# Gated mix of attention and FFN for one token: 384 columns of a w_down block as strips of 16 rows, and two more blocks in the early sum

## Chip, cores and metric

The kernel runs on one core of a Trainium2 chip. The metric is the device time of one execution in microseconds (us), as the median of several runs.

## What is computed

One token x of 1024 numbers goes through attention over a cache and through a gated FFN; a sigmoid gate mixes the two. All is float32. In short, from the reference:

```python
# x (1,1,1024); k_cache, v_cache (1,4,65536,128); wq (1024,4096); wo (4096,1024)
g = sigmoid((x * gate_w).sum(-1))
a = softmax(q @ k.T * 128**-0.5) @ v @ wo          # 32 heads, 8 to each of 4 cached groups
r = x @ w_r
y = (silu(x @ w_gate) * (x @ w_up)) @ w_down       # w_gate, w_up (1024,3584); w_down (3584,1024)
out = g * a + (1 - g) * (x + y * sigmoid(r))
```

The router picks one of one token, so every token is routed. The caches are 268 MB, and all inputs together 346 MB, each read once.

## The kernel before

**The stream.** All inputs are loaded by one queue, SP's, in the order in which they are used, into three large buffers, kbuf, vbuf and wbuf, each of 128 partitions by 64 KB. SP waits until TensorE has finished with a buffer and then issues the next transfer into it (`load`, lines 108 to 111). Keys go to kbuf, values to vbuf, the matrices wq, wo and most of w_down to wbuf. The host packs everything after the caches into one array, `tail`, with one row for each partition.

**Attention** runs over 4 groups of heads in 4 steps each; per group wo is applied and summed into T, a PSUM tile of 128 x 512 (T is never cleared until the end; four quarters of 32 partitions hold partial sums, the first and third for columns 0 to 511 of the output, the second and fourth for columns 512 to 1023; `tiles`, line 151, deals the blocks round).

**FFN.** w_gate and w_up arrive in halves in kbuf and vbuf (lines 210 to 225, two passes). After each pass seven small matmuls S <- row, sel4 (line 224) spread the 3584 results over 128 partitions by 28 columns, one column for each block of 128 rows of w_down. VectorE forms the hidden vector from it, in `hid` and, with zeros around each number so that it can serve as a weight of 32 columns, in `hp` (line 384).

**The end, w_down in 28 blocks** of 128 rows by 1024 columns. Blocks 0 to 15 come in wbuf: VectorE sums blocks 0 to 5 into `t` (the early sum, lines 393 to 398), TensorE takes 6 to 15 into T (line 231), then t (line 233), then blocks 16 to 23 from kbuf (lines 234 to 237). VectorE copies T to `join` (line 400). The rest goes into a second, narrow PSUM tile Y of 128 x 64: blocks 24 and 25, then join itself by a matmul with `selj` that adds T's quarters, then block 26, then block 27 in two pieces (lines 244 to 263). A block in T takes two matmuls of 512 columns, a block in Y sixteen of 64. VectorE transposes Y into `fin` and SP stores it (lines 402 to 404).

TensorE's instructions run in the order written; a wait holds up all behind it. The parts of w_down that go to kbuf are issued together, and TensorE waits for each by its own semaphore `s_part`:

```python
    parts = [4 * D, 4 * D, 2 * D, D] + [4 * CW * (r1 - r0) for r0, r1 in PIECES]
    for k, n in enumerate(parts):
        to = at - down - W
        load(kb[:, to : to + n], tail[:, at : at + n], s_part[k], 0 if k else FFN + 4)
```

Of the kernel before, what the change touches and what calls it, by code (L numbers as in the profile page):

```python
# [4 lines left out]
AF = mybir.ActivationFunctionType  # L5
# [11 lines left out]
W = 16384  # L17
KB = D // P
FB = F // P
FR = F // 8  # L20
FQ = FB // 4
SCALE = DH ** -0.5
XN = 32
JOIN = 24
SUMS = 6
R4 = 4
CW = D // 16
PIECES = ((0, 3), (3, 4))

# [20 lines left out]

def gated_mix(nc, k_t, v_t, wq0, wo_wq, tail, out):
    pe, dve, act, pool = (
# [10 lines left out]
    def sb(name, *shape):  # L63
        return nc.alloc_sbuf_tensor(name, (P, *shape), F32)[:]
# [3 lines left out]
    if nc.sbuf_base % 256:  # L68
# [7 lines left out]
    xp, qp, op, hp = sb("xp", KB, 32), sb("qp", 4 * (32 + HG)), sb("op", HG, 32), sb("hp", FB, 36)  # L76
    hid = sb("hid", FB)
    sel, sel8, sel4, selq, selj = (
        sb("sel", 32), sb("sel8", HG), sb("sel4", 4), sb("selq", 2), sb("selj", 2, 36),
    )  # L80
# [6 lines left out]
    nbs = nb0, nb1  # L87
    xr, fin = sb("xr", KB), sb("fin", 2 * 32)

# [34 lines left out]
    half = KB // 2 * F  # L124
    down = at + 4 * half
    for dst, n, sem, after in (
# [107 lines left out]
    for k in range(2):  # L234
        p.wait_ge(s_part[k], 16)
        d2 = kb[:, 4 * k * D : 4 * (k + 1) * D].rearrange("p (b n) -> p b n", n=D)
        ins = tiles(T, [hp[:, 16 + 4 * k + b, 3:35] for b in range(4)], d2, False, k == 1)
    join_ready = pe(ins)

    def y_row(j, r, lhs, rhs, first=False, last=False):  # L240

        return mm(y[32 * j : 32 * j + 32, :], lhs[:, 3 - r : 35 - r], rhs, first, last)

    later = kb[:, 8 * D : 11 * D].rearrange("p (b j r n) -> p b j r n", b=3, j=4, r=R4)
    for b in range(3):
        if b != 1:
            p.wait_ge(s_part[(2, 0, 3)[b]], 16)
        for r in range(R4):
            for j in range(4):
                y_row(j, r, hp[:, JOIN + b, :], later[:, b, j, r, :], b == r == 0)  # L250
        if b == 1:
            event()
            joined = join.rearrange("p (j r n) -> p j r n", j=2, r=R4)
            for r in range(R4):
                for j in range(4):
                    y_row(j, r, selj[:, j // 2, :], joined[:, j % 2, r, :])
    at = 11 * D
    for k, (r0, r1) in enumerate(PIECES):
        p.wait_ge(s_part[4 + k], 16)
        for r in range(r0, r1):  # L260
            for j in range(4):
                ins = y_row(j, r, hp[:, FB - 1, :], kb[:, at : at + CW], False, r == R4 - 1)
                at += CW
    y_done = pe(ins)

# [95 lines left out]
    for u in range(2):  # L361
        act.wait(pe, FFN + 3 * u + 2)
        if u:
            act.wait(dve)
        a.activation(
            row.rearrange("p (e n) -> p e n", e=2), R.rearrange("p (e n) -> p e n", e=2)[:, :, :FR], AF.Copy
        ).then_inc(to_pe, 1)
        cols = FFN + 3 * u + 3
        if u == 0:
            act.wait(pe, cols)  # L370
            act(a.activation(hid, S[:, :FB], AF.Exp, scale=-1.0))
# [17 lines left out]
    d(v.tensor_mul(hid, S[:, :FB], hid))
    dacc, h = t, hid.rearrange("p (m j) -> p j m", j=4)  # L390
# [50 lines left out]
```

## Time and profile before

| | |
|---|---|
| median of 3 runs | 805.45 us (805.37 to 805.81) |
| the profiled execution | 805.7 us, span 804.4 us |
| TensorE matmuls busy | 396.7 us, 49% of the span |
| VectorE, ScalarE, GpSimd busy | 82.2, 24.9, 2.7 us |
| read from HBM | 346.05 MB, 430 GB/s over the span |
| mean granted clock of TensorE | 0.739 of 2.4 GHz |

The span runs from the first to the last instruction of the program; the profiled execution's time is 1.3 us longer than its span. Busy shares are means over the whole span; the change touches mainly its last 60 us, and times below are counted from the start of the span. TensorE (PE) has its weight loads listed apart (PEld). A float32 matmul appears as two records, so "x40" in the trace is 20 matmuls.

### The profile page before, as it was taken

Reading aid. Unit: us, or ns where it says so; the run is one execution under the profiler, and the core shown is the slowest. Engines: PE = TensorE matmul, PEld = TensorE weight load, DVE = VectorE, ACT = ScalarE, POOL = GpSimd, SP = SyncE. Lnnn points to the kernel's source line nnn. Section 1 sums busy time; section 2 is a strip of 40 time slices with the busy share of each in tenths; the row PEclk is TensorE's granted clock in tenths of the full one; section 3 lists DMA queues with packets and bytes.
Section 4 is the critical chain, followed back from the end, with each engine's and each line's share of the span. In section 5 each row is a group of like instructions: output and inputs, shape, how many; then the busy total and the mean of one; then the engine's idle time right before and its main releaser. Section 6 shows DMA issues by size and latency. Waiting matters only on the chain. (4 is left out here: it accounts for less than half of the span.)

```text
span 804.4 us, 6296 instructions
## 1 busy us (share of the span) xinstructions
PE 396.7 (49%) x2932; PEld 124.3 (15%) x2932; DVE 82.2 (10%) x159; ACT 24.9 (3%) x49; POOL 2.7 (0%) x12
## 2 busy tenths in 40 slices
PE   3444554455544444455445455455444454545556
PEld 1111111111111111111111111111111111111222
DVE  1010101010001010100101010100101010100004
ACT  0000000000000000000000000000000000000000
POOL 1000000000000000000000000000000000000000
PEclk9777677677676776776776777777777777777768
DMA  9999999999999999999999999999999999999997
GB/s 415 420 418 466 417 420 466 417 417 463 424 417 460 427 417 460 427 417 460 427 417 456 430 417 453 433 417 450 433 420 443 440 420 430 437 449 417 451 422 320
DMA packets 7061, 346.13 MB, mean 430 GB/s; under 512 B 912, under 2 KB 1040, under 8 KB 1296
## 3 DMA queue, kind: packets, MB, share of 16 engines
q1 hardware_dynamic: 7056, 346.05, 99.4%
q8 instruction: 4, 0.07, 0.0%
q14 instruction: 1, 0.01, 0.0%
HBM read 346.05 MB, written 0.00 MB: 430 GB/s over the span
## 5 line engine op out<-in xcount | busy, mean ns | idle before, releaser
L149 PE MATMUL S<-kbuf,qp 128*32 128x512 f32 x1024 | 145.2, 730 | 155.6 <-PEq L146 155.6
L149 PE MATMUL A<-vbuf,pt 128*32 128x512 f32 x1024 | 145.2, 730 | 132.3 <-PEq L146 132.3
L149 PEld LDWEIGHTS S<-kbuf,qp 128*32 128x32 f32 x1024 | 40.1, 131 | 257.4 <-issue 257.4
L149 PEld LDWEIGHTS A<-vbuf,pt 128*32 128x32 f32 x1024 | 40.1, 131 | 224.4 <-issue 224.4
L322 DVE TENSOR_REDUCE m<-S 128x1 f32<-128x1024 f32 x16 | 19.6, 1224 | 291.3 <-PE S L149 291.3
L149 PE MATMUL T<-wbuf,op 128*32 128x512 f32 x128 | 21.9, 847 | 24.5 <-PEq L146 24.5
L341 DVE SCALAR_TENSOR_TENSOR acc<-acc,alpha,A 128x512 f32<-128x512 f32 x12 | 9.0, 748 | 169.1 <-PE A L149 169.1
L149 PE MATMUL R<-vbuf,xp 128*32 128x448 f32 x128 | 17.6, 721 | 16.3 <-PEq L146 16.3
L149 PE MATMUL R<-kbuf,xp 128*32 128x448 f32 x128 | 17.5, 716 | 15.6 <-PEq L146 15.6
L334 ACT ACTIVATE t<-S,nb 128x1024 f32<-128x1024 f32 x16 | 17.6, 1099 | 196.8 <-DVE nb L327 196.8
L338 DVE STREAM_TRANSPOSE pt<-t 128x1024 f32<-128x1024 f32 x16 | 19.8, 1239 | 5.1 <-ACT t L334 5.1
L149 PE MATMUL M<-mg,heads 128*128 128x16 f32 x32 | 5.9, 259 | 27.3 <-PEq L143 27.3
L333 ACT ACTIVATE alpha<-nb 128x1 f32<-128x1 f32 x12 | 3.5, 294 | 449.5 <-DVE nb L330 449.5
L149 PE MATMUL R<-wbuf,xp 128*32 128x512 f32 x128 | 16.1, 647 | 0.0
L149 PEld LDWEIGHTS T<-wbuf,op 128*32 128x32 f32 x128 | 5.7, 148 | 37.5 <-issue 37.5
L149 PEld LDWEIGHTS M<-mg,heads 128*128 128x128 f32 x32 | 4.8, 188 | 41.4 <-issue 41.4
L149 PE MATMUL T<-wbuf,hp 128*32 128x512 f32 x40 | 6.1, 771 | 7.5 <-DMA wbuf<-in_tail 7.5
L149 PEld LDWEIGHTS R<-vbuf,xp 128*32 128x32 f32 x128 | 5.4, 140 | 28.6 <-issue 28.6
L149 PEld LDWEIGHTS R<-kbuf,xp 128*32 128x32 f32 x128 | 5.4, 140 | 27.1 <-issue 27.1
L149 PE MATMUL T<-join 128*128 128x512 f32 x2 | 2.0, 1126 | 13.9 <-PEq L143 13.9
L343 DVE COPY acc<-A 128x512 f32<-128x512 f32 x4 | 2.8, 691 | 59.7 <-PE A L149 59.7
L394 DVE SCALAR_TENSOR_TENSOR t<-wbuf,hid,t 128x1024 f32<-128x1024 f32 x6 | 7.7, 1285 | 7.3 <-DMA wbuf<-in_tail 7.1
(74 smaller groups left out, 80.5 us busy)
## 6 DMA issues: line engine op xcount, KB each, us to landing
kbuf<-in_tail SPq DMA_DIRECT2D x2, 7168.0 KB, 31.0
vbuf<-in_tail SPq DMA_DIRECT2D x2, 7168.0 KB, 29.5
wbuf<-in_wq SPq DMA_DIRECT2D x1, 4112.0 KB, 12.6
wbuf<-in_tail SPq DMA_DIRECT2D x1, 4096.0 KB, 38.0
kbuf<-in_tail SPq DMA_DIRECT2D x2, 2048.0 KB, 34.3
kbuf<-in_tail SPq DMA_DIRECT2D x1, 1024.0 KB, 38.5
kbuf<-in_tail SPq DMA_DIRECT2D x1, 512.0 KB, 39.3
kbuf<-in_tail SPq DMA_DIRECT2D x1, 384.0 KB, 39.8
```

The source lines that it names most:

```text
L149: return p.matmul(o, w, r, start=first, stop=last)
L322: d(v.tensor_reduce(m1, S, AX.X, ALU.max))
L333: act(a.activation(alpha, was, AF.Exp, bias=now, scale=-1.0))
L334: act(a.activation(t, S, AF.Exp, bias=now, scale=SCALE, accum_out=sums if i else l1))
L338: tell_pe(v.transpose(pt, t))
L341: d(v.scalar_tensor_tensor(acc, acc, alpha, A, op0=ALU.mult, op1=ALU.add))
L343: d(v.tensor_copy(acc, A))
L394: ins = v.scalar_tensor_tensor(dacc, wb[:, b * D : (b + 1) * D], h[:, 0, b : b + 1], dacc, op0=ALU.mult, op1=ALU.add)
```

## The change

In block 23 of w_down the columns 0 to 383 no longer come with the rest of the block. The host cuts the 128 rows of this piece into eight strips of 16 rows and packs them in a new input, `low`, of four rows with four partitions' data in each. One transfer puts them side by side on partitions 0 to 15 of kbuf; its leading dimension of four has it carried by four DMA engines. It is the first of the transfers into kbuf behind wbuf. Eight matmuls with 16 rows and 384 columns add the strips into T. So that the hidden numbers of block 23 also stand on partitions 0 to 15, eight matmuls of one column are added to each FFN pass, and `hp` and `hid` have 36 columns in place of 28 (they are laid out as four groups of nine).

Blocks 24 and 25 are added into T, ahead of the copy to join, and no longer into Y. Y starts with join. The pieces of the stream behind wbuf are cut anew: the strips, blocks 16 to 19, blocks 20 to 22 and the rest of 23, blocks 24 and 25, block 26 with three quarters of 27, and the last quarter of 27. The strips and blocks 16 to 19 are taken ahead of the early sum t, which stood ahead of block 16.

```diff
-    parts = [4 * D, 4 * D, 2 * D, D] + [4 * CW * (r1 - r0) for r0, r1 in PIECES]
-    for k, n in enumerate(parts):
-        to = at - down - W
-        load(kb[:, to : to + n], tail[:, at : at + n], s_part[k], 0 if k else FFN + 4)
+    n = SUB * MOVED
+    load(kb[:LOW, LAST : LAST + n], low[:, : OWN * n].rearrange("e (q n) -> e q n", q=OWN), s_part[0], FFN + 4)
+    to = 0
+    for k, n in enumerate((4 * D, 4 * D - MOVED, 2 * D, 2 * D - 4 * CW, 4 * CW)):
+        load(kb[:, to : to + n], tail[:, at : at + n], s_part[k + 1])
         at += n
+        to += n
...
         for m in range(FQ):
-            ins = mm(S[:, 4 * m : 4 * m + 4], row[:, m * P : (m + 1) * P], sel4)
+            mm(S[:, 4 * m : 4 * m + 4], row[:, m * P : (m + 1) * P], sel4)
+        j, m = divmod(SPLIT, FQ)
+        for q in range(SUB):
+            at = m * P + q * LOW
+            ins = mm(S[:, FB + q : FB + q + 1], row[:, at : at + P], sel4[:, j : j + 1])
...
     event()
     p.wait_ge(s_down, 16)
+    p.wait_ge(s_part[0], 16)
     d1 = wb.rearrange("p (b n) -> p b n", n=D)
-    tiles(T, [hp[:, b, 3:35] for b in range(SUMS, 16)], d1[:, SUMS:, :], False, False)
+    tiles(T, [flat(hb(b)) for b in range(SUMS, 16)], d1[:, SUMS:, :], False, False)
+    for q in range(SUB):
+        j = q % 2 * 2
+        mm(
+            T[32 * j : 32 * j + 32, :MOVED], flat(hp[:LOW, q % 4 * HB + FQ + q // 4, :]),
+            kb[:LOW, LAST + q * MOVED : LAST + (q + 1) * MOVED], False, False,
+        )
+    p.wait_ge(s_part[1], 16)
+    tiles(T, [flat(hb(16 + b)) for b in range(4)], kb[:, : 4 * D].rearrange("p (b n) -> p b n", n=D), False, False)
     event()
     tiles(T, [ones[:, :32]], t.unsqueeze(1), False, False)
...
+    p.wait_ge(s_part[2], 16)
+    split = flat(hb(SPLIT))
+    at = 7 * D
+    mm(T[:32, MOVED:], split, kb[:, at : at + 512 - MOVED], False, False)
+    mm(T[32:64, :], split, kb[:, at + 512 - MOVED : at + D - MOVED], False, False)
+    at += D - MOVED
+    tiles(T, [flat(hb(20 + b)) for b in range(3)], kb[:, 4 * D : 7 * D].rearrange("p (b n) -> p b n", n=D), False, False)
+    p.wait_ge(s_part[3], 16)
+    join_ready = pe(
+        tiles(T, [flat(hb(24 + b)) for b in range(2)], kb[:, at : at + 2 * D].rearrange("p (b n) -> p b n", n=D), False, True)
+    )
```

On TensorE the end of the program stood like this before (from the first w_down matmul on; T and Y are the PSUM tiles, kbuf and wbuf hold w_down, hp the hidden vector, t the early sum):

```order
L149 MATMUL T<-wbuf,hp 32x512 x20
L149 MATMUL T<-t,ones 32x512 x2
L149 MATMUL T<-kbuf,hp 32x512 x16
L149 MATMUL Y<-kbuf,hp 32x64 x32
L149 MATMUL Y<-join,selj 32x64 x16
L149 MATMUL Y<-kbuf,hp 32x64 x32
```

and now it stands like this, from the same place on:

```order
L157 MATMUL T<-wbuf,hp 32x512 x20
L157 MATMUL T<-kbuf,hp 32x384 x8
L157 MATMUL T<-kbuf,hp 32x512 x8
L157 MATMUL T<-t,ones 32x512 x2
L157 MATMUL T<-kbuf,hp 32x128
L157 MATMUL T<-kbuf,hp 32x512 x11
L157 MATMUL Y<-join,selj 32x64 x16
L157 MATMUL Y<-kbuf,hp 32x64 x32
```

The eight strips and eight matmuls of blocks 16 to 19 have moved between wbuf and t, T has 27 matmuls on kbuf and 1 of 128 columns where it had 16 in all with t behind wbuf, and 32 matmuls into Y ahead of join are gone.

On SP, the queue of transfers, the last ones before the store were (destination <- source, partitions x numbers):

```order
L111 DMA wbuf<-in_tail 128x16384
L111 DMA kbuf<-in_tail 128x4096 x2
L111 DMA kbuf<-in_tail 128x2048
L111 DMA kbuf<-in_tail 128x1024
L111 DMA kbuf<-in_tail 128x768
L111 DMA kbuf<-in_tail 128x256
```

and are now:

```order
L118 DMA wbuf<-in_tail 128x16384
L118 DMA kbuf<-in_low 16x1x3072
L118 DMA kbuf<-in_tail 128x4096
L118 DMA kbuf<-in_tail 128x3712
L118 DMA kbuf<-in_tail 128x2048
L118 DMA kbuf<-in_tail 128x1792
L118 DMA kbuf<-in_tail 128x256
```

The strips stand directly behind wbuf; the 128-row transfers behind them carry 384 numbers a row less in all.

## Rows read from the trace of the kernel before

**Rows 1.** The page: busy time, share of the span and instructions of each engine; then the DMA share in tenths and GB/s in 40 equal slices of the span; then two of the DMA queues, with packets, MB and share of the 16 engines' time.

```profile
PE 396.7 (49%) x2932; PEld 124.3 (15%) x2932; DVE 82.2 (10%) x159; ACT 24.9 (3%) x49; POOL 2.7 (0%) x12
...
PE   3444554455544444455445455455444454545556
...
DMA  9999999999999999999999999999999999999997
GB/s 415 420 418 466 417 420 466 417 417 463 424 417 460 427 417 460 427 417 460 427 417 456 430 417 453 433 417 450 433 420 443 440 420 430 437 449 417 451 422 320
...
q1 hardware_dynamic: 7056, 346.05, 99.4%
q8 instruction: 4, 0.07, 0.0%
```

**Rows 2.** The windows, one full stretch and the end: from and to, length, then busy us and instructions of PE, PEld, DVE, ACT and POOL, and last the granted clock of TensorE, the mean busy share of the 16 DMA engines and GB/s.

```profile
740.00:755.00 15.00, 8.52 (x70) 3.71 (x66) 0.93 (x4) 1.11 (x2) 0.00 (x0) 0.72 1.00 433
...
799.60:800.00 0.40, 0.40 (x17) 0.30 (x18) 0.00 (x0) 0.00 (x0) 0.00 (x0) 1.00 0.91 336
800.00:800.40 0.40, 0.40 (x43) 0.40 (x36) 0.30 (x1) 0.00 (x0) 0.00 (x0) 1.00 0.33 128
...
801.20:801.60 0.40, 0.40 (x44) 0.40 (x37) 0.00 (x0) 0.00 (x0) 0.00 (x0) 1.00 0.15 54
801.60:802.00 0.40, 0.40 (x35) 0.33 (x28) 0.00 (x0) 0.00 (x0) 0.00 (x0) 1.00 0.05 18
802.00:803.00 1.00, 0.60 (x35) 0.44 (x32) 0.25 (x1) 0.00 (x0) 0.00 (x0) 1.00 0.00 0
```

**Rows 3.** The DMA issues of w_down's last parts: destination <- source, queue, count, KB of each, median us from issue to landing.

```profile
kbuf<-in_tail SPq DMA_DIRECT2D x1, 1024.0 KB, 38.5
...
kbuf<-in_tail SPq DMA_DIRECT2D x1, 384.0 KB, 39.8
...
kbuf<-in_tail SPq DMA_DIRECT2D x1, 128.0 KB, 39.7
```

**Rows 4.** The timeline of the end: start, length, engine, line, operation, out<-in, shapes, count of records, and in brackets the idle time before and what ended it.

```profile
760.31 2.70 SPq L111 DMA_DIRECT2D kbuf<-in_tail  x6
...
787.50 7.89 DVE L394 SCALAR_TENSOR_TENSOR t<-wbuf,hid,t 128x1024 f32<-128x1024 f32 x6 [7.08 <-DMA wbuf<-in_tail]
...
787.52 6.12 PE L149 MATMUL T<-wbuf,hp 128*32 128x512 f32 x40 [7.49 <-DMA wbuf<-in_tail]
...
795.54 0.62 PE L149 MATMUL T<-t,ones 128*32 128x512 f32 x2 [1.90 <-PEq L143]
...
795.57 0.62 PE L149 MATMUL T<-kbuf,hp 128*32 128x512 f32 x2
...
795.97 0.62 PE L149 MATMUL T<-t,ones 128*32 128x512 f32 x2
...
796.02 4.00 PE L149 MATMUL T<-kbuf,hp 128*32 128x512 f32 x30
...
800.10 0.69 DVE L400 COPY join<-T 128x512 f32<-128x512 f32 x1 [4.71 <-PE T L149]
...
800.94 0.65 PE L149 MATMUL Y<-join,selj 128*32 128x64 f32 x32
...
801.38 1.22 PE L149 MATMUL Y<-kbuf,hp 128*32 128x64 f32 x64
802.67 0.25 DVE L402 STREAM_TRANSPOSE fin<-Y 128x64 f32<-128x64 f32 x1 [1.88 <-PE Y L149]
```

**Rows 5.** The same timeline around the small matmuls of the FFN passes.

```profile
751.44 8.81 PE L149 MATMUL R<-kbuf,xp 128*32 128x448 f32 x64 [5.36 <-PEq L146]
...
778.34 1.70 PE L149 MATMUL S<-sel,row 128*128 128x4 f32 x14 [1.12 <-PEq L143]
```

**Rows 6.** The waits: engine, tile and line, what it waited for, us in total, times, longest.

```profile
DVE xp L293 <- DMA wbuf<-in_wq: 8.5, 1, 8.5
```

**Rows 7.** The timeline of TensorE's weight loads for the w_down matmuls on wbuf, columns as in rows 4.

```profile
789.23 0.20 PEld L149 LDWEIGHTS T<-wbuf,hp 128*32 128x32 f32 x4 [0.66 <-issue]
790.09 0.20 PEld L149 LDWEIGHTS T<-wbuf,hp 128*32 128x32 f32 x4 [0.66 <-issue]
790.90 0.12 PEld L149 LDWEIGHTS T<-wbuf,hp 128*32 128x32 f32 x4 [0.62 <-issue]
791.33 0.12 PEld L149 LDWEIGHTS T<-wbuf,hp 128*32 128x32 f32 x4 [0.31 <-issue]
...
792.62 0.12 PEld L149 LDWEIGHTS T<-wbuf,hp 128*32 128x32 f32 x4 [0.31 <-issue]
```

**Rows 8.** The windows for the same matmuls, columns as in rows 2.

```profile
787.60:790.80 3.20, 3.20 (x16) 0.71 (x20) 3.13 (x3) 0.00 (x0) 0.00 (x0) 0.50 1.04 445
790.90:793.60 2.70, 2.70 (x28) 0.60 (x20) 2.63 (x3) 0.00 (x0) 0.00 (x0) 1.00 0.93 401
```

**Rows 9.** The timeline of TensorE's weight loads in two FFN bursts: the first of each, and where their distance changes.

```profile
751.40 0.23 PEld L149 LDWEIGHTS R<-kbuf,xp 128*32 128x32 f32 x8 [5.41 <-issue]
...
756.64 0.18 PEld L149 LDWEIGHTS R<-kbuf,xp 128*32 128x32 f32 x4 [0.52 <-issue]
...
768.27 0.23 PEld L149 LDWEIGHTS R<-vbuf,xp 128*32 128x32 f32 x8 [8.82 <-issue]
...
774.02 0.14 PEld L149 LDWEIGHTS R<-vbuf,xp 128*32 128x32 f32 x4 [0.30 <-issue]
```

More of the change, by code (lines that the diff above doesn't have):

```diff
@@ L23 @@
 XN = 32
-JOIN = 24
+JOIN = 26
+SPLIT = 23
 SUMS = 6
-R4 = 4
+RY = 4
+BY = 8 // RY
 CW = D // 16
-PIECES = ((0, 3), (3, 4))
+LOW = 16
+OWN = 4
+SUB = P // LOW
+HB = 7 + SUB // 4
+MOVED = 384
+LAST = 12 * D
 class Flow:
@@ L48, in own, with gated_mix @@
         self.wait(self)
-def gated_mix(nc, k_t, v_t, wq0, wo_wq, tail, out):
+def gated_mix(nc, k_t, v_t, wq0, wo_wq, tail, low, out):
     pe, dve, act, pool = (
@@ L75, in gated_mix @@
     wb = wb[:, :W]
-    xp, qp, op, hp = sb("xp", KB, 32), sb("qp", 4 * (32 + HG)), sb("op", HG, 32), sb("hp", FB, 36)
-    hid = sb("hid", FB)
+    xp, qp, op, hp = sb("xp", KB, 32), sb("qp", 4 * (32 + HG)), sb("op", HG, 32), sb("hp", 4 * HB, 32 + RY)
+    hid = sb("hid", 4 * HB)
     sel, sel8, sel4, selq, selj = (
-        sb("sel", 32), sb("sel8", HG), sb("sel4", 4), sb("selq", 2), sb("selj", 2, 36),
+        sb("sel", 32), sb("sel8", HG), sb("sel4", 4), sb("selq", 2), sb("selj", 2, 32 + RY),
     )
@@ L87, in gated_mix @@
     nbs = nb0, nb1
-    xr, fin = sb("xr", KB), sb("fin", 2 * 32)
+    xr, fin = sb("xr", KB), sb("fin", BY * 32)
     def ps(name, n=512):
@@ L124, in gated_mix @@
     half = KB // 2 * F
-    down = at + 4 * half
     for dst, n, sem, after in (
@@ L149, in mm, with hb, flat @@
         return p.matmul(o, w, r, start=first, stop=last)
+    def hb(b):
+        return hp[:, b // FQ * HB + b % FQ, :]
+    def flat(h):
+        return h[:, RY - 1 : RY + 31]
     def tiles(o, lhs, rhs, first, last, n=512):
@@ L223, in gated_mix, with y_rows @@
         for m in range(FQ):
-            ins = mm(S[:, 4 * m : 4 * m + 4], row[:, m * P : (m + 1) * P], sel4)
+            mm(S[:, 4 * m : 4 * m + 4], row[:, m * P : (m + 1) * P], sel4)
[3 more added lines that the diff above has]
+            ins = mm(S[:, FB + q : FB + q + 1], row[:, at : at + P], sel4[:, j : j + 1])
         pe(ins)
     pe.n = FFN + 6
+    def y_rows(rhs, lhs, lo=0, hi=D // 4, first=False, last=False):
+        n = D // 4 // RY
+        for r in range(RY):
+            c0, c1 = max(lo, r * n), min(hi, r * n + n)
+            for j in range(4 if c0 < c1 else 0):
+                ins = mm(
+                    y[32 * j : 32 * j + 32, c0 - r * n : c1 - r * n], lhs(j)[:, RY - 1 - r : RY + 31 - r],
+                    rhs(j)[:, c0 - lo : c1 - lo], first and r == 0, last and r == RY - 1,
+                )
+        return ins
@@ L232, in gated_mix @@
+    p.wait_ge(s_part[1], 16)
+    tiles(T, [flat(hb(16 + b)) for b in range(4)], kb[:, : 4 * D].rearrange("p (b n) -> p b n", n=D), False, False)
     event()
     tiles(T, [ones[:, :32]], t.unsqueeze(1), False, False)
[L234 to L264, printed above, removed]
+    p.wait_ge(s_part[2], 16)
[3 more added lines that the diff above has]
+    mm(T[32:64, :], split, kb[:, at + 512 - MOVED : at + D - MOVED], False, False)
@@ new lines, in gated_mix, with columns @@
+    at += D - MOVED
[3 more added lines that the diff above has]
+        tiles(T, [flat(hb(24 + b)) for b in range(2)], kb[:, at : at + 2 * D].rearrange("p (b n) -> p b n", n=D), False, True)
+    )
+    at += 2 * D
+    def columns(at, n):
+        return lambda j: kb[:, at + j * n : at + (j + 1) * n]
+    event()
+    y_rows(lambda j: join.rearrange("p (j n) -> p j n", j=2)[:, j % 2, :], lambda j: selj[:, j // 2, :], first=True)
@@ L267, in gated_mix @@
+    p.wait_ge(s_part[4], 16)
+    y_rows(columns(at, D // 4), lambda j: hb(JOIN))
+    at += D
+    edge = D // 4 - CW
+    y_rows(columns(at, edge), lambda j: hb(FB - 1), hi=edge)
+    p.wait_ge(s_part[5], 16)
+    y_done = pe(y_rows(columns(at + 4 * edge, CW), lambda j: hb(FB - 1), lo=edge, last=True))
     pool(gp.memset(ident, 0.0))
@@ L370, in gated_mix @@
             act.wait(pe, cols)
-            act(a.activation(hid, S[:, :FB], AF.Exp, scale=-1.0))
+            act(a.activation(hid, S[:, : 4 * HB], AF.Exp, scale=-1.0))
             dve.wait(act)
@@ L376, in gated_mix @@
             dve.own()
-            d(v.tensor_mul(hid, S[:, :FB], hid))
+            d(v.tensor_mul(hid, S[:, : 4 * HB], hid))
             dve.own()
@@ L388, in gated_mix @@
             )
-    d(v.tensor_mul(hid, S[:, :FB], hid))
+    d(v.tensor_mul(hid, S[:, : 4 * HB], hid))
     dacc, h = t, hid.rearrange("p (m j) -> p j m", j=4)
@@ L401, in gated_mix @@
     dve.wait(pe, y_done)
-    d(v.transpose(fin.rearrange("p (r b) -> p b r", b=2), y))
+    d(v.transpose(fin.rearrange("p (r b) -> p b r", b=BY), y))
     sp.wait_ge(dve.sem, dve.n)
@@ L413 @@
     wq = a["A_wq"].reshape(P, KB, G, HG * DH).transpose(2, 0, 1, 3)
-    turned = lambda w: w.reshape(-1, 4, 32, R4, 2).transpose(0, 1, 3, 4, 2)
+    turned = lambda w: w.reshape(-1, 4, 32, D // P).transpose(0, 1, 3, 2)
     wo = turned(a["A_wo"]).reshape(G, HG, P, D).transpose(0, 2, 1, 3)
     down = turned(a["B_w_down"]).reshape(FB, P, D).transpose(1, 0, 2)
-    last = down[:, -1].reshape(P, 4, R4, CW)
+    last = down[:, -1].reshape(P, 4, D // 4)
+    moved = down[:, SPLIT, :MOVED].reshape(SUB, LOW // OWN, OWN, MOVED).transpose(1, 2, 0, 3).reshape(LOW // OWN, -1)
     vecs = np.zeros((P, XN), np.float32)
@@ L426 @@
             [wo[-1].reshape(P, -1), a["B_w_gate"].reshape(P, -1), a["B_w_up"].reshape(P, -1)]
-            + [down[:, :-1].reshape(P, -1)]
-            + [last[:, :, r0:r1].transpose(0, 2, 1, 3).reshape(P, -1) for r0, r1 in PIECES],
+            + [down[:, :SPLIT].reshape(P, -1), down[:, SPLIT:-1].reshape(P, -1)[:, MOVED:]]
+            + [x.reshape(P, -1) for x in (last[:, :, :-CW], last[:, :, -CW:])],
             axis=1,
         ),
+        "low": np.pad(moved, ((0, 0), (0, D))),
     }
```

6 lines of the change are left out of this document (3 added, 3 removed).

## Prediction

> **What bounds the kernel now.** I read the page first. Its slices show the DMA engines busy in nine tenths or more of every slice but the last, at 415 to 466 GB/s, and TensorE mostly in four or five tenths [rows 1]. So 346 MB are streamed without a pause, and only two things can move the time: the bytes that the slowest of the 16 engines carries, and what follows its last byte.
>
> The second view is the windows. In a full stretch 433 GB/s are moved, 27.1 GB/s by each engine; in the last microseconds the share falls to 0.33 between 800.0 and 800.4, to 0.15, to 0.05, and is zero from 802.0 [rows 2]. A third of 16 is five: eleven engines are done by about 800.2, the other five go on, the last ones for almost 2 us. The landings agree: six transfers are issued in the 2.70 us from 760.31, and the last, of 128 KB, lands 39.7 us after its issue, at about 802.3; the one before it lands 39.8 us after its own, at about 801.9 [rows 3, 4].
>
> The third view is TensorE's timeline of the end [rows 4]. The w_down matmuls on wbuf start at 787.52 and end at 793.64. Then TensorE is idle for 1.90 us, until VectorE's early sum, six steps that end at 795.39, may be added. T ends at 800.02, its copy to join runs from 800.10 for 0.69, the Y matmuls end at 802.60, and the transpose starts at 802.67 [rows 4]. So the last matmuls end 0.3 us behind the last landing, and the transpose and the store behind them do not change. The reader should see two clocks that end together: the stream, and TensorE, with 1.9 us of slack in its middle.
>
> **The stream.** Each of the 128 rows loses 384 columns, 1536 bytes. An engine carries eight rows, so twelve engines lose 12 KB, which is 0.45 us at 27.1 GB/s. The other four carry four rows of 12 KB of the new input, 48 KB, 1.82 us, and end 1.82 - 0.45 = 1.37 us later than they did. If these four are among the eleven that end near 800.2, they now end at about 801.6, and the slowest engine ends at 801.85 in place of 802.3: a gain of 0.45 on the stream. The Trainium skill ("DMA: Bandwidth & Descriptors", section on why a semaphore rises by 16) says that a transfer gets the largest number of engines that divides both leading sizes, here 4 and 16; no row shows such a transfer yet.
>
> **FFN and start.** Eight more matmuls of one column stand in each pass behind the seven that take 1.70 us [rows 5], so at most 1.70 x 8/7 = 1.95 us a pass. In the first pass TensorE then waits 5.36 us for kbuf, in the second VectorE waits 7.08 us for wbuf [rows 4, 5]: cost nothing; without that cover 1.95. A larger zeroing of hp adds under a microsecond to POOL's 2.7 in all, against 8.5 us in which VectorE waits for the first load [rows 1, 6]: nothing; wider operations on hid stand under the same 7.08. SP issues as many transfers behind wbuf as before, over 20 us ahead of their use.
>
> **The wait that moves.** TensorE now waits for wbuf and for the strips before its first w_down matmul, and all of T is queued behind it. The strips lie behind wbuf on four engines. On an early engine wbuf is done 2 us before 787.5, so they land at 787.5 - 2 + 1.82 = 787.3: nothing. On the latest engine they would land at 789.3: a rival below.
>
> **TensorE's sum.** A matmul into 32 rows of T uses one of four column groups, and four go side by side: weight loads come in fours, 0.86 us apart until 790.09 and 0.43 us apart from 790.90 [rows 7], where the granted clock goes from 0.50 to 1.00 [rows 8], from 1.2 to 2.4 GHz. Each matmul is two such passes, so a 512-column one costs its group 0.86 us at 2.4 GHz. Before, a group got five from wbuf and, in the first two groups, one for the early sum and four from kbuf: 5 x 0.86 = 4.3 from 795.54, and the row ends at 800.02, 0.18 later, the run-out of the last. That the groups run on independently is seen at 795.57: matmuls on kbuf start between the two passes on t, which can only be the third and fourth group [rows 4].
>
> Now the first group. From wbuf it is free at 792.62 + 2 x 0.43 = 793.48 as before. Then come four of the eight strips (the strips use groups one and three alone) of 384 columns, no such shape is in the trace; by columns each is 0.75 x 0.86 = 0.64, together 2.57. Bounds: half of it if one pass did, 1.29; and double, 5.15, if the two groups took turns; I take 2.57, since the nearest rows, those on t and kbuf, show groups side by side. Then two from blocks 16 to 19 (1.72), one for the early sum (0.86, ready since 795.4), 128 columns of block 23 (0.21), two from blocks 20 to 22 (1.72), one from block 24 (0.86). Sum 7.94: free at 801.42, with the run-out 801.60, against 800.02. The slack of 1.9 us is filled, and nothing on the way waits for data: the piece with block 24 takes the place of one that landed 38.5 us after its issue, at about 799.7 [rows 3], and the group comes to it at 800.56.
>
> Behind T: copy at 801.68 for 0.69, the first join matmul 0.15 later, as before, at 802.52. Sixteen Y matmuls take 0.44 (the join row starts at 800.94, the next at 801.38) and run out in 0.21 more [rows 4]. The 48 that are left, all data landed, take 3 x 0.44 + 0.21 = 1.53: end at 804.05. Before it was 802.60. So +1.45 us in this execution; dropping 32 Y matmuls for blocks 24 and 25 is counted in it, since they stood ahead of the stream's end.
>
> To that comes the clock. Of the 6.12 us on wbuf the first 3.3 ran at 1.2 GHz [rows 8], and before, the 1.9 us of slack absorbed it; now each microsecond more at 1.2 GHz costs half of one. Other bursts in this trace ran longer before the passes got faster: 751.40 to 756.64 is 5.2 us, 768.27 to 774.02 is 5.7 us [rows 9]. The mean of the three is 4.7, 1.4 more than here, half of which is 0.7. I take 0.6, with bounds of -0.4 and +1.2. **Sum: 1.45 + 0.6 = 2.05 us.** The profiled execution took 805.7 with a span of 804.4; the median of the runs is 805.45, 0.25 under it, and I add the sum to the median: 807.5.
>
> **Rivals.**
> - *TensorE is not the bound.* T would have to end by about 800.0, 1.6 us sooner than summed: with the strips at one pass (1.29 saved) and a slightly earlier clock, or the clock at 2.4 GHz from the start (1.66 saved). Then the end follows the stream. The piece ahead of the last lands at 801.5, the 28 Y matmuls behind it take 7 x 0.11 = 0.77 and the last four 0.11, end at about 802.4: 0.2 to 0.45 sooner than before, 805.1. For it speaks the stream's share of 1.00 everywhere; against it that every term of the sum but the strips is a row. Chance 0.25.
> - *The groups stop at the strips.* If groups two and four may not run on while groups one and three take the strips, group two starts block 16 at 796.05 and has 7 matmuls of 0.86 left, 802.07, and with two run-outs of 0.16 to 0.18 about 802.4 in place of 801.42: another 0.95 us, 808.45. The Trainium skill ("TensorEngine Tiling (Array Packing)", Key Properties) says that a change of tiling mode, not of tile alone, drains TensorE, and a strip of 16 rows has another mode than 128 rows; by that rule it is this case. No row of before has two such shapes without a wait between them. Chance 0.25.
> - *One of the four engines is a late one.* Then the strips land between 788.3 and 789.3, TensorE starts 0.8 to 1.8 us later and T ends as much later, 808.3 to 809.3. No row names the engines; by count alone it would be likely (four of 16 beside five late ones), yet one of the mildly late ones would cost little. Chance 0.15.
>
> **How the numbers follow.** My case has 0.35. It gives 807.5, with its own range of 806.5 to 808.7 from the clock. A measurement of this kernel tells about 0.2%, 1.6 us, from no change: below 807.06 nothing is slower by that. Of my case about three quarters lie above, 0.26; the next two rivals lie above but for a little, 0.38: slower 0.64. The first rival and the rest of my case are within it: 0.33. For a gain over 1.6 us the stream would have to lose all its lateness at once: 0.03. The range must hold the first rival, since it has more than 2 in 10: 805.0 to 809.0 leaves out the upper half of the third rival and little else.
>
> **What would show it.** Right: in TensorE's timeline no gap near 794, a row of sixteen 128x384 passes there, T running past 801, join copied at 801.7 or later, three blocks of Y without a gap, and DMA share zero while they run. The strips in fours 0.32 us apart support the 2.57. Wrong: T ending near 800 and a wait of Y for kbuf (first rival); no block 16 matmul before the last strip ended (second); a first w_down matmul well behind wbuf's landing, VectorE starting its early sum before it (third). One of the four instruction packets [rows 1], if it fell on one of the four engines near the end, would upset the first rival's sum as well.

## The result, and the profile after

The changed kernel takes 810.02 us as the median of six executions (808.83 to 810.33), against 805.46 (805.37 to 805.95) before: a ratio of 1.0052, with a 95% interval of 1.0039 to 1.0065. It is slower by 4.56 us, where 2.05 were forecast; the range to 809.0 does not hold it. Five further executions in a later series had a median of 809.16 (808.85 to 809.38; ratio 1.0046, 1.0032 to 1.0060). One execution of experiment 7 ran in a slower state of the chip (838.67 us) and is in none of the figures below.

The profiled execution took 808.83 us with a span of 807.5. The page's first part answers to [rows 1]:

```profile
PE 408.1 (51%) x2924; PEld 131.4 (16%) x2924; DVE 82.3 (10%) x159; ACT 25.0 (3%) x49; POOL 3.0 (0%) x12
```

TensorE is busy for 11.4 us longer, in part because it ran at the lower clock for longer (below). The timeline of the end, with the columns of [rows 4]:

```profile
776.94 5.64 PE L157 MATMUL S<-sel,row 128*128 128x4 f32 x30 [1.12 <-PEq L151]
...
787.37 7.89 DVE L427 SCALAR_TENSOR_TENSOR t<-wbuf,hid,t 128x1024 f32<-128x1024 f32 x6 [4.38 <-DMA wbuf<-in_tail]
...
788.40 6.05 PE L157 MATMUL T<-wbuf,hp 128*32 128x512 f32 x40 [5.81 <-DMA kbuf<-in_low]
...
794.38 4.62 PE L157 MATMUL T<-kbuf,hp 16*32 16x384 f32 x32
...
798.82 1.03 PE L157 MATMUL T<-t,ones 128*32 128x512 f32 x4
...
799.68 3.60 PE L157 MATMUL T<-kbuf,hp 128*32 128x128 f32 x24
...
803.35 0.69 DVE L433 COPY join<-T 128x512 f32<-128x512 f32 x1 [8.09 <-PE T L157]
...
804.63 1.10 PE L157 MATMUL Y<-kbuf,hp 128*32 128x64 f32 x64
805.79 0.25 DVE L435 STREAM_TRANSPOSE fin<-Y 128x64 f32<-128x64 f32 x1 [1.75 <-PE Y L157]
```

The reader should see three things. VectorE starts its early sum at 787.37, when wbuf is there, but TensorE starts at 788.40, released by the strips (in_low): 0.88 us later than in [rows 4]. From then on the timeline shows TensorE without a gap until T ends. And the copy to join starts at 803.35, 3.25 us later than before and 1.67 later than forecast; what follows it takes as long as forecast (2.38 us to the last Y matmul, 2.37 forecast).

The weight loads of the same execution, with the columns of [rows 7], show how the column groups take the strips:

```profile
790.94 0.22 PEld L157 LDWEIGHTS T<-wbuf,hp 128*32 128x32 f32 x4 [0.63 <-issue]
791.69 0.14 PEld L157 LDWEIGHTS T<-wbuf,hp 128*32 128x32 f32 x4 [0.53 <-issue]
...
793.40 0.13 PEld L157 LDWEIGHTS T<-wbuf,hp 128*32 128x32 f32 x4 [0.29 <-issue]
794.38 0.14 PEld L157 LDWEIGHTS T<-kbuf,hp 16*32 16x32 f32 x4 [0.84 <-issue]
794.73 0.11 PEld L157 LDWEIGHTS T<-kbuf,hp 16*32 16x32 f32 x2 [0.21 <-issue]
...
796.34 0.11 PEld L157 LDWEIGHTS T<-kbuf,hp 16*32 16x32 f32 x2 [0.21 <-issue]
797.08 0.16 PEld L157 LDWEIGHTS T<-kbuf,hp 128*32 128x32 f32 x8 [0.62 <-issue]
```

From 794.73 the strips come in pairs 0.32 us apart, the distance that was forecast. But nothing else is loaded beside them: block 16, whose data had landed by 793.2, begins at 797.08 on all groups at once. Groups two and four stood still from the end of wbuf's work to the last strip. From 797.08 group two has seven matmuls of 0.86 left, 6.02, and the run-out of 0.18: 803.28, and the copy starts at 803.35. At both ends of the strips the weights also come late: the first strips' 0.98 us behind wbuf's last four, where fours stand 0.43 apart, and block 16's 0.74 behind the last pair, where pairs stand 0.32 apart. Since loads otherwise come a pass ahead, TensorE lost less than that: the strips could have started at 793.40 + 2 x 0.43 = 794.26 and block 16 at 796.34 + 2 x 0.32 = 796.98, so each started about 0.1 us late.

The windows show the clock, with the columns of [rows 2]:

```profile
777.00:777.90 0.90, 0.90 (x9) 0.90 (x9) 0.00 (x0) 0.00 (x0) 0.00 (x0) 1.00 1.01 437
778.00:782.50 4.50, 4.50 (x22) 4.50 (x22) 0.00 (x0) 0.00 (x0) 0.00 (x0) 0.50 0.84 364
788.40:791.50 3.10, 3.10 (x16) 0.88 (x20) 2.99 (x4) 0.00 (x0) 0.00 (x0) 0.50 0.97 414
791.60:794.30 2.70, 2.70 (x28) 0.67 (x20) 2.63 (x3) 0.00 (x0) 0.00 (x0) 1.00 0.99 425
...
802.00:803.00 1.00, 1.00 (x9) 0.11 (x1) 0.00 (x0) 0.00 (x0) 0.00 (x0) 1.00 0.01 4
```

The w_down matmuls began at 1.2 GHz and went to 2.4 GHz after 3.1 to 3.2 us, about as before (3.3). From 802.0 to 803.0, while T is still being summed, the stream is all but over (a DMA share of 0.01).

Last, the times at which the 16 DMA engines completed a transfer, as the trace records them on its semaphore:

```
wbuf, before         785.46 to 785.91 (12 engines)  786.43 787.10 787.29 787.48
wbuf, after          785.36 to 785.81 (12 engines)  786.45 787.01 787.06 787.35
strips, after        787.22 787.37 787.59 788.27 (4 engines)
last piece, before   800.17 to 800.62 (12 engines)  801.13 801.71 801.97 802.24
last piece, after    799.62 to 800.02 (9 engines)   801.12 801.26 801.43 801.48 801.58 801.80 802.48
```

1.82 us, the forecast time for an engine's strips, taken off the strips' row gives 785.40, 785.55, 785.77 and 786.45: three early engines and the first of the late ones.

### The profile page after: what moved, and what is told of

The parts are those of the page before. It is cut to its first block, busy times and chain, and to the rows that moved or that the text cites. A ratio compares the mean times of both kernels' runs of the same rounds, so it can differ in the third digit from the quotient of the medians.

```text
span 807.5 us, 6281 instructions
## 1 busy us (share of the span) xinstructions
PE 408.1 (51%) x2924; PEld 131.4 (16%) x2924; DVE 82.3 (10%) x159; ACT 25.0 (3%) x49; POOL 3.0 (0%) x12
## 5 line engine op out<-in xcount | busy, mean ns | idle before, releaser
L157 PE MATMUL A<-vbuf,pt 128*32 128x512 f32 x1024 | 147.6, 741 | 131.5 <-PEq L154 131.5
L157 PE MATMUL R<-kbuf,xp 128*32 128x448 f32 x128 | 15.1, 632 | 9.1 <-PEq L154 9.1
L157 PE MATMUL S<-sel,row 128*128 128x1 f32 (+1 forms) x60 | 9.9, 300 | 2.3 <-PEq L151 2.3
L157 PEld LDWEIGHTS S<-sel,row 128*128 128x128 f32 x60 | 9.8, 259 | 3.8 <-issue 3.8
```

## Experiments

A simple sum carries through all of them: from the first w_down matmul to the copy to join is the row on wbuf plus a rest. In the changed kernel the rest is 803.35 - 788.40 - 6.05 = 8.90 us. The row on wbuf takes 4.50 us where it runs at 2.4 GHz throughout (seen below) and longer by half of the time spent at 1.2 GHz.

**1. The wait for the strips behind wbuf.**

```diff
     p.wait_ge(s_down, 16)
-    p.wait_ge(s_part[0], 16)
...
     tiles(T, [flat(hb(b)) for b in range(SUMS, 16)], d1[:, SUMS:, :], False, False)
+    p.wait_ge(s_part[0], 16)
     for q in range(SUB):
```

> The changed kernel, with the wait for the strips moved from ahead of the first w_down matmul on wbuf to just ahead of the first strip. Theory (TensorE's chain into T sets the end, and 0.9 us of it is the strips' late landing): the matmuls on wbuf start with wbuf's landing, near 787.5 in place of 788.4, T ends 0.5 to 0.9 us sooner, 809.1 to 809.5. Rival (the stream's own end is what is late): no change, 810.0.

Measured: 808.43 us (808.10 to 809.25), ratio 1.0035 (1.0022 to 1.0049). Its timeline:

```profile
787.88 6.13 PE L157 MATMUL T<-wbuf,hp 128*32 128x512 f32 x40 [4.71 <-DMA wbuf<-in_tail]
...
802.92 0.69 DVE L433 COPY join<-T 128x512 f32<-128x512 f32 x1 [7.17 <-PE T L157]
```

TensorE starts with wbuf's landing, and the rest is 802.92 - 787.88 - 6.13 = 8.91, unchanged. The late strips are a cost by themselves; the strips' own landing at 788.88 hides behind wbuf's matmuls. The median is lower than the 809.1 to 809.5 expected from a median of 810.0; against the profile of the changed kernel, 808.83, this profile (808.43) is 0.40 shorter, and its start lies 0.52 earlier.

**2. Strips as matmuls over 128 rows.** Partitions 16 to 127 get zeros as weights, so the sum is the same and the columns are the same; only the number of rows differs.

```diff
-            T[32 * j : 32 * j + 32, :MOVED], flat(hp[:LOW, q % 4 * HB + FQ + q // 4, :]),
-            kb[:LOW, LAST + q * MOVED : LAST + (q + 1) * MOVED], False, False,
+            T[32 * j : 32 * j + 32, :MOVED], flat(hp[:, q % 4 * HB + FQ + q // 4, :]),
+            kb[:, LAST + q * MOVED : LAST + (q + 1) * MOVED], False, False,
...
+            d(v.tensor_scalar_mul(hid[:, FB:], hid[:, FB:], mask))
```

> The changed kernel, with the eight strip matmuls over all 128 rows, the same shape of weights as their neighbours; the hidden numbers of the other 112 rows are set to zero beforehand, so the sum is the same. Theory A (the change of tile shape stops column groups two and four while the strips run): blocks 16 to 19 start in these groups beside the strips, T ends about 1.0 to 1.1 us sooner, 808.9 to 809.1. Theory B (matmuls start strictly in order, whatever their shape, once two groups are taken): no change, 810.0.

Measured: 808.97 (807.59 to 809.67), ratio 1.0036 (1.0022 to 1.0049). The profiled execution was the slowest of these. Its timeline, and its weight loads around the strips:

```profile
788.72 7.45 PE L158 MATMUL T<-wbuf,hp 128*32 128x512 f32 x40 [5.78 <-DMA kbuf<-in_low]
795.98 4.05 PE L158 MATMUL T<-kbuf,hp 128*32 128x384 f32 x30
...
804.19 0.69 DVE L437 COPY join<-T 128x512 f32<-128x512 f32 x1 [8.68 <-PE T L158]
```

```profile
797.60 0.13 PEld L158 LDWEIGHTS T<-kbuf,hp 128*32 128x32 f32 x2 [0.19 <-issue]
797.92 0.16 PEld L158 LDWEIGHTS T<-kbuf,hp 128*32 128x32 f32 x6 [0.19 <-issue]
```

At 797.92 six loads come where the strips alone have two: block 16 begins on the free groups while strips still run. It does so beside the last pair of strips only, 0.64 us; the pairs ahead of it run alone here too. The rest is 804.19 - 788.72 - 7.45 = 8.02, 0.88 less than with 16 rows. What the profile also shows is a late rise of the clock: the row on wbuf lasts 7.45, 1.4 us more than in the changed kernel, and takes the gain back in this execution. The median lies in the range expected of theory A.

**3. Both.** Edits 1 and 2 together.

> The changed kernel with both the late wait and the strips over 128 rows. The runs so far fit one sum: TensorE needs 13.3 us at 2.4 GHz from the first matmul on wbuf to T's end with 16-row strips and 12.4 with 128-row strips, and half of what it spends at 1.2 GHz on top. From 787.6 that gives T's end at 801.5 to 803.0 for 3.0 to 6.0 us at 1.2 GHz, and the time is T's end plus 5.55: 807.1 to 808.6, middle 807.8. Rival (the two gains are one and the same, the later of two waits): not below the 808.4 of the late wait alone.

Measured: 807.46 (806.85 to 808.64), ratio 1.0025 (1.0016 to 1.0033).

```profile
787.72 5.83 PE L158 MATMUL T<-wbuf,hp 128*32 128x512 f32 x40 [4.72 <-DMA wbuf<-in_tail]
...
801.59 0.69 DVE L437 COPY join<-T 128x512 f32<-128x512 f32 x1 [5.99 <-PE T L158]
```

The rest is 8.04, the start is that of wbuf: both causes are there, and they add. The median lies in the expected range.

**4. A warm clock.** Five matmuls of 256 columns into the scratch tile M ahead of the w_down matmuls, nothing else.

```diff
+    for _ in range(5):
+        mm(M[:, :256], ones, row[:, :256])
     event()
```

> The changed kernel with five added matmuls of 256 columns, whose result nobody reads, in the idle time of TensorE before wbuf lands. Theory (the median lies 1.2 us above the profiled execution because the clock rises at another time in each, and 3.2 us at 1.2 GHz cost 1.6 us even there): the w_down matmuls on wbuf run at 2.4 GHz from the start, T ends 1.6 us sooner than in the profile of the changed kernel, the runs scatter less, median 807.2 to 807.9. Rival (the scatter has another cause): 810.0 less 1.6, 808.4, with the same scatter.

Measured: 808.82 (807.61 to 809.55), ratio 1.0035 (1.0022 to 1.0049). Two rows of its timeline, and its windows:

```profile
788.21 4.50 PE L157 MATMUL T<-wbuf,hp 128*32 128x512 f32 x40 [1.61 <-DMA kbuf<-in_low]
...
803.31 0.69 DVE L435 COPY join<-T 128x512 f32<-128x512 f32 x1 [8.04 <-PE T L157]
```

```profile
788.20:792.00 3.80, 3.79 (x36) 1.42 (x40) 3.69 (x4) 0.00 (x0) 0.00 (x0) 1.00 1.00 428
792.70:796.10 3.40, 3.40 (x26) 1.03 (x28) 2.53 (x2) 0.00 (x0) 0.00 (x0) 1.00 0.97 414
796.20:799.50 3.30, 3.30 (x16) 0.79 (x10) 0.00 (x0) 0.00 (x0) 0.00 (x0) 0.50 0.99 411
```

The row on wbuf takes 4.50 us here, 1.55 less. But behind the strips the clock fell to 1.2 GHz until about 799.5, and the rest is 803.31 - 788.21 - 4.50 = 10.60 in place of 8.90. What the row gained was lost again, and neither expected time came.

**5. All three edits.**

> The same with the added matmuls ahead of wbuf's landing. In the run with these matmuls alone the clock was at 2.4 GHz for the matmuls on wbuf but fell for 3.4 us at 796.2, behind the strips. Theory A (16-row strips count little as activity; 128-row ones keep the clock up): 2.4 GHz throughout, TensorE reaches blocks 24 and 25 before they land, T ends 1.1 us behind their landing of 800.0 to 800.6, 806.6 to 807.3, with little scatter. Theory B (the fall has nothing to do with the strips): the clock falls here too, 1.7 us more, 808.3.

Measured: 806.84 (806.61 to 807.37), ratio 1.0014 (1.0005 to 1.0023). The median is in the range of theory A, but the profile does not show the 2.4 GHz throughout that it assumed: in the profiled execution, the slowest one, the extra matmuls ended at 784.15, the row on wbuf began at 787.64, and the clock fell at 788.30, so that the row took 6.20 us; the rest was 8.04. How often the extra matmuls helped in the others no profile shows.

**6. Blocks 24 and 25 in T, no strips**: the kernel before with that part of the change alone.

```diff
-        ins = tiles(T, [hp[:, 16 + 4 * k + b, 3:35] for b in range(4)], d2, False, k == 1)
+        tiles(T, [hp[:, 16 + 4 * k + b, 3:35] for b in range(4)], d2, False, False)
+    p.wait_ge(s_part[2], 16)
+    d2 = kb[:, 8 * D : 10 * D].rearrange("p (b n) -> p b n", n=D)
+    ins = tiles(T, [hp[:, 24 + b, 3:35] for b in range(2)], d2, False, True)
...
```

The matmuls of these two blocks into Y (at the dots) are gone, and Y starts with join.

> The kernel before, with blocks 24 and 25 added into T ahead of the copy to join, and nothing else of the change. Theory (behind the landing of blocks 24 and 25 stand one matmul of 0.86 us, its run-out 0.18, the copy 0.08 + 0.69, the first join matmul 0.15 and three blocks of Y 1.53): landing at 799.7 gives T's end near 800.9 and the last Y matmul near 803.3, 0.7 us later than before, 806.1. Rival (taking 32 narrow matmuls out of Y pays for it): 805.0 to 805.5.

Measured: 806.60 (806.20 to 807.02), ratio 1.0011 (1.0002 to 1.0020).

```profile
800.81 0.69 DVE L400 COPY join<-T 128x512 f32<-128x512 f32 x1 [5.56 <-PE T L149]
...
802.09 1.10 PE L149 MATMUL Y<-kbuf,hp 128*32 128x64 f32 x64
803.25 0.25 DVE L402 STREAM_TRANSPOSE fin<-Y 128x64 f32<-128x64 f32 x1 [1.75 <-PE Y L149]
```

T ends 0.71 later than in [rows 4] and the transpose starts 0.58 later, though TensorE still has its gap ahead of the early sum. That is the timeline that was expected, but the median lies 0.94 above that of the kernel before in the same series (805.66), 0.5 more than expected. So this part alone costs about 0.9 us.

**7. The strips alone**: the changed kernel with blocks 24 and 25 back in Y, ahead of join.

```diff
     p.wait_ge(s_part[3], 16)
-    join_ready = pe(
-        tiles(T, [flat(hb(24 + b)) for b in range(2)], kb[:, at : at + 2 * D].rearrange("p (b n) -> p b n", n=D), False, True)
-    )
-    at += 2 * D
+    for b in range(2):
+        y_rows(columns(at, D // 4), lambda j: hb(24 + b), first=b == 0)
+        at += D
...
```

> The changed kernel with blocks 24 and 25 added into Y ahead of join, as before: the strips and the new order of pieces alone. By the sum: 13.3 less the 0.86 us of a block, from 788.3, with 3.0 to 6.0 us at 1.2 GHz: T's end 802.2 to 803.7, time 807.8 to 809.3, so that the strips make up some 3 us of the 4.6. Rival (the early adding of blocks 24 and 25 is the main cost): 806.5 or less.

Measured: 809.21 as the median of five executions (808.62 to 810.35), ratio 1.0048 (1.0035 to 1.0061), in the expected range. Its timeline:

```profile
788.17 6.49 PE L157 MATMUL T<-wbuf,hp 128*32 128x512 f32 x40 [5.89 <-DMA kbuf<-in_low]
...
802.66 0.69 DVE L434 COPY join<-T 128x512 f32<-128x512 f32 x1 [7.76 <-PE T L157]
```

The strips make by far the larger part of the loss: 3.48 us alone, against the 805.73 of the kernel before in the same series. With the 0.94 of experiment 6 that is 4.42, where the changed kernel lost 4.56 in its first series and 3.74 in the later one. Taking two blocks out of T shortens the rest by 0.90 (802.66 - 788.17 - 6.49 = 8.00). In this execution a longer row on wbuf (6.49) takes half of that back, and the store ends 2.1 us behind the transpose's start in place of 1.7.

**8. The strips three times.** Every strip is added three times over, so 24 matmuls stand where 8 did; once with 16 rows and once with 128 rows as in experiment 2. The output holds the strips' share three times.

```diff
-    for q in range(SUB):
+    for q in [*range(SUB)] * 3:
```

> The changed kernel with its eight strip matmuls of 16 rows issued three times over (block 23's strips are then counted three times). By the sum the added sixteen cost 8 x 0.64 = 5.15 us at 2.4 GHz. Theory A (matmuls of 16 rows in two column groups do not keep the clock up): in the 7.7 us of strips the clock falls to 1.2 GHz, and the time is 815.5 us or more. Theory B (any matmul does): no fall, T ends 18.45 us plus half of the 3 to 6 us at 1.2 GHz behind the first matmul on wbuf, 813.7 to 815.4.

> The same three times over with the strips over 128 rows. Both theories: no fall of the clock while the strips run; by the sum 17.55 us plus half of the time at 1.2 GHz, 812.8 to 814.5. If the clock falls here as well, the rows of a matmul are not what matters, and the two column groups that stand idle may be.

Measured, one execution each: 821.27 us with 16 rows, 813.72 with 128 rows. Weight loads with 16 rows:

```profile
800.76 0.11 PEld L157 LDWEIGHTS T<-kbuf,hp 16*32 16x32 f32 x2 [0.21 <-issue]
801.19 0.18 PEld L157 LDWEIGHTS T<-kbuf,hp 16*32 16x32 f32 x2 [0.31 <-issue]
801.83 0.18 PEld L157 LDWEIGHTS T<-kbuf,hp 16*32 16x32 f32 x2 [0.46 <-issue]
...
804.39 0.18 PEld L157 LDWEIGHTS T<-kbuf,hp 16*32 16x32 f32 x2 [0.46 <-issue]
805.81 0.20 PEld L157 LDWEIGHTS T<-kbuf,hp 128*32 128x32 f32 x8 [1.24 <-issue]
```

and the windows, first with 16 rows, then with 128 (first while strips alone ran, then at their end):

```profile
802.00:805.00 3.00, 3.00 (x12) 0.73 (x9) 0.00 (x0) 0.00 (x0) 0.00 (x0) 0.50 0.00 0
```

```profile
798.00:801.00 3.00, 3.00 (x21) 1.21 (x19) 0.00 (x0) 0.00 (x0) 0.00 (x0) 1.00 0.81 326
801.00:803.70 2.70, 2.70 (x27) 1.21 (x26) 0.00 (x0) 0.00 (x0) 0.00 (x0) 1.00 0.06 23
```

TensorE was busy without a break in both, and in the first two of these windows on two column groups alone. With 16 rows the clock fell, while nothing but such matmuls ran, and from 801.19 the pairs came 0.64 apart; with 128 rows the pairs stayed 0.32 apart and the clock stayed at 2.4 GHz. Matmuls of 16 rows did not keep the clock up. That the clock fell just as the stream ended is not the reason: in experiment 4 it fell with the DMA share at 0.97 to 0.99. In the changed kernel itself the clock stayed at 2.4 GHz through and behind the eight strips. Both times are as expected, 815.5 or more and 812.8 to 814.5.

**9. All repairs.** Experiment 7 and the late wait; 128-row strips; seven extra matmuls; and each strip cut into halves (columns 320 to 511 and 512 to 703 of the block), so that all four groups take strips.

```diff
+    half_m = MOVED // 2
     for q in range(SUB):
-        j = q % 2 * 2
+        for e in range(2):
+            j = q % 2 * 2 + e
...
```

> The strips with all that the runs so far point to: blocks 24 and 25 in Y as before, the wait for the strips behind the matmuls on wbuf, the strips over 128 rows, cut so that all four column groups share them (columns 320 to 703 of block 23 in place of 0 to 383), and seven added matmuls ahead of wbuf. By the sum TensorE needs 10.3 us at 2.4 GHz for T, so T ends by 799 to 800 and the stream sets the end. Theory (one of the four engines that carry the strips is itself 0.9 us late, so their 1.37 us more cancel what the others save): 805.4 to 805.8, the same as before within 0.05%. Rival (the stream gains its 0.45 us once TensorE is out of the way): 805.0 to 805.3.

Measured: 806.51 (806.26 to 807.00), ratio 1.0012 (1.0003 to 1.0021): neither theory's time.

```profile
800.05 0.69 DVE L444 COPY join<-T 128x512 f32<-128x512 f32 x1 [4.84 <-PE T L158]
...
802.14 1.10 PE L158 MATMUL Y<-kbuf,hp 128*32 128x64 f32 x64 [0.58 <-DMA kbuf<-in_tail]
```

T is as early as before, and now Y waits for the stream. The change also merged block 26 with three quarters of 27 into one piece; it lands at 802.09 with 64 passes behind it. In the changed kernel that had been covered, since T was later (join copied at 803.35).

**10. That piece cut in two**, as before the change.

```diff
-    for k, n in enumerate((4 * D, 4 * D - MOVED, 2 * D, 2 * D - 4 * CW, 4 * CW)):
+    for k, n in enumerate((4 * D, 4 * D - MOVED, 2 * D, D, D - 4 * CW, 4 * CW)):
```

> The last wait was on the second to last piece of the weights: block 26 and three quarters of block 27 in one piece, which landed at 802.09 us, with 64 matmuls (1.10 us) behind it, where the kernel before has block 26 in a piece that lands at 800.90 and only 32 to 48 matmuls left behind 801.90. This kernel is the one with all repairs, with that piece cut in two as before, and nothing else. If the coarser piece is what remained: Y's last matmul ends near 802.65 as in [rows 4], 805.3 to 805.8 us, about 0.9 below the uncut version, and the strips cost nothing once they don't hold up the early sum. Rival, that T's end (copy at 800.05) and the Y matmuls on the sum bind instead: no change, 806.2 to 806.7.

Measured: 806.23 (805.99 to 806.94), ratio 1.0009 (1.0000 to 1.0018): the rival's time.

```profile
788.61 4.50 PE L158 MATMUL T<-wbuf,hp 128*32 128x512 f32 x40
...
802.57 0.65 PE L158 MATMUL Y<-kbuf,hp 128*32 128x64 f32 x32 [0.20 <-DMA kbuf<-in_tail]
803.29 0.25 DVE L447 STREAM_TRANSPOSE fin<-Y 128x64 f32<-128x64 f32 x1 [2.19 <-PE Y L158]
```

The extra matmuls ran to 788.68 here and held up the start, yet T did not bind: Y waited for kbuf. The row on wbuf takes 4.50 us as in experiment 4, and behind these strips of 128 rows on all four groups the clock stays at 2.4 GHz. The cut did what it should, 32 passes in place of 64 behind the landing, but the landing came at 802.52, against 801.90 before the change, and the transpose is late by the same 0.62. In this execution the store adds 0.2 more (it ends 1.96 us behind the transpose's start, before 1.73); together they are its 806.57 against 805.7. Neither branch of the expectation named that. The last piece completed at 802.86 on one engine, 0.84 after the next; its strips had completed 0.81 after the other three's. So with T out of the way the end follows the engine that carries strips and was late already. That this engine is the whole remaining 0.76 us is argued from one profile, not shown by an edit. No version beat the kernel before.

**11. The changed kernel again**, four times, for the spread of its executions.

> The changed kernel once more, for a second profile: the profiled execution of the changed kernel took 808.83 us, the median of its runs was 810.02. Theory: here the clock rises later than 3.2 us after the first matmul on wbuf, or falls again behind the strips, and the time is T's end plus 5.55, with T's end at the first matmul plus 13.3 plus half of the time at 1.2 GHz. Rival (something other than the clock varies): a longer time with the same clock.

> The changed kernel unchanged, to see what its slower executions (810 us) have that the two profiled ones (808.8 and 808.9) have not. Theory, a later rise of the clock: in every profile the copy to join starts at the first w_down matmul's start + 13.3 us + half of the time at 1.2 GHz, the time is that start + 5.5 us, and an execution near 810 shows 5 to 6 us at 1.2 GHz where the two showed 3.2. Median 809.2 to 810.2. Rival, that the slower executions start later (strips or wbuf later by 1 us) with the same 3.2 us.

> The same kernel, another profiled execution; the same expectation.

> The same kernel, another profiled execution; the same expectation.

Measured: 808.92; 809.16 as a median (808.85 to 809.38); 808.97; 809.35. The last one's timeline:

```profile
788.50 6.46 PE L157 MATMUL T<-wbuf,hp 128*32 128x512 f32 x40 [5.86 <-DMA kbuf<-in_low]
...
803.85 0.69 DVE L433 COPY join<-T 128x512 f32<-128x512 f32 x1 [8.58 <-PE T L157]
```

The five profiles of this kernel start between 788.33 and 788.50, and the rest is 8.89 to 8.91 in all. The four from 808.8 to 809.0 have a row on wbuf of 6.03 to 6.12, this one of 6.46, and it is 0.4 us slower: the clock, not the start. The later median, 809.16, is just under the 809.2 to 810.2 expected, and an execution near 810 was not profiled. The first kernel of experiment 8, which is the changed kernel as far as the strips, shows that a longer row occurs:

```profile
788.25 7.40 PE L157 MATMUL T<-wbuf,hp 128*32 128x512 f32 x40 [6.02 <-DMA kbuf<-in_low]
```

With such a row the changed kernel would take 808.83 + 7.40 - 6.05 = 810.2 us. That the executions near 810 had one stays an inference.

## Why the prediction was wrong

The direction and the bound were right. Two steps failed: the wait that moves, where the strips' landing was put at nothing, and TensorE's sum, where groups two and four were to run beside the strips. The runs showed 0.88 us for the first and 0.87 us for the second. Both stood among the rivals with a price near that, but as alternatives to the sum; both came true and were added to it.

- *The sum over group one: right.* The strips' passes were priced by their columns at 0.32 us, and so they came. Its rest is 801.68 - 787.52 - 6.12 = 8.04 us, and experiments 3 and 5, with the two rivals repaired, show 8.04. Experiment 3 takes 807.46 us; the forecast was 807.5. The agreement of the times includes a clock term that its profile did not need (row on wbuf 5.83, against 6.12 before), so part of it is luck.
- *"The groups stop at the strips" (0.25): true.* Priced at 0.95; the rest is 8.90 with 16 rows and 8.02 to 8.04 with 128, so 0.87. By the weight loads 0.65 of it is group two's seven matmuls behind the strips, 6.02, in place of group one's 5.37 (7.94 less the strips' 2.57), and 0.12 and 0.10 are the late starts of the strips and of block 16. The prediction took its main value from rows on t and kbuf, which have one shape among them and so could not bear on it. The Trainium skill ("TensorEngine Tiling (Array Packing)", Key Properties) states that changing the tiling mode drains TensorE; the trace agrees: nothing ran beside the strips, and 0.12 and 0.10 us were lost at their two ends.
- *"One of the four engines is a late one" (0.15): true, in its mild form.* 0.88 us, inside the 0.8 to 1.8 given. The chance was too small: the prediction counted five late engines of 16, and four drawn from 16 miss five others in fewer than one case of five (11/16 x 10/15 x 9/14 x 8/13 = 0.18). The completions show four late ones, by which it is 0.27. In each of the fifteen profiles with strips one of the four completed 0.56 to 0.95 us behind the third. The Trainium skill ("DMA: Bandwidth & Descriptors", the section on why a semaphore rises by 16) led to four engines; the strips' four completions agree.
- *The stream: half right.* The engines without strips end about 0.5 us earlier, as forecast (0.45). The slowest, though, is now the late one with strips: 801.13 + 1.37 = 802.50, found at 802.48, so the stream ends 0.24 later and not 0.45 sooner. This also takes the ground from the first rival's 805.1: experiments 9 and 10 removed T as the bound and stayed at 806.2 to 806.5.
- *FFN: the size wrong, the cover right.* The fifteen small matmuls take 5.64 us, against at most 3.65 forecast (1.70 + 1.95), since the clock fell to 1.2 GHz by 778.0; where it did not fall, in experiment 9, they took 3.48. VectorE still waited 4.38 us for wbuf, so nothing was paid.
- *The clock: right in kind, its size unsettled.* In the five profiles of the changed kernel the term is between -0.1 and +0.35; forecast was +0.6 (-0.4 to +1.2). The row of 7.40 in experiment 8 would be +1.28.

In the profiled execution the parts close: load 1.45, late strips 0.88, stopped groups 0.87, together 3.20, clock -0.07; the profiles differ by 808.83 - 805.7 = 3.13. The median of the first six executions lies another 1.2 higher, and the median before 0.2 under its profile, which makes the 4.56. The clock can give the 1.2, but no profile of this kernel caught it, so its cause stays open; the second five lie 0.3 higher.

## What to carry to other kernels

Rivals that can occur together have to be summed with the main case, not weighed against it: here 1.45 + 0.88 + 0.87 was the answer in the profiles, and each part had been priced. Before a transfer is given to a few engines to save bytes on the others, read each engine's completion of the transfers around it: what counts is the latest of the few. And matmuls with another number of rows, in the middle of matmuls that run side by side, cost their neighbours time as well here; filling them up to the same rows with zeros cost no column more and removed that.

## What was not expected of the hardware

- Matmuls of 16 rows did not keep TensorE's clock at 2.4 GHz although it was busy without a gap: pairs 0.32 us apart became 0.64 apart at 801.19 in the first kernel of experiment 8, and with 128 rows stayed at 0.32 throughout (one execution each; experiments 4 and 10 point the same way).
- At the change of shape not even the weights were loaded ahead: the first strips' loads start with their matmuls (794.38 in both views), two pairs at once, and block 16's come as two fours at once (797.08), where loads in the middle of a row come a pass ahead.
- Extra matmuls ahead of a burst are no sure remedy for a slow start: the row on wbuf took 4.50 us in the profiles of experiments 4 and 10, but 6.20 in those of experiments 5 and 9, where they ended at 784.15 and 785.15, the row began at 787.64 and 787.34, and the clock fell 0.7 us into it. In experiment 10 they ran to 788.68 and so held up the row by 1.2 us.
